# First layer of two more chunks by seven block products, with activations and weights parked in DRAM

## The chip, the cores and the metric

The kernel runs on one core of a Trainium2 chip. The metric is the device time of one execution in microseconds. Five engines run side by side, each through its own list of instructions in order: PE (matrix products; PEld is its weight load, which overlaps the products), DVE (VectorE), ACT (ScalarE), POOL (GpSimd) and SP, which here only issues DMA transfers. Engines wait for each other by semaphores.

## The reference

Masked attention over 8 batches and 8 heads of 576 tokens and 64 dimensions, then a feed-forward layer with softplus on the 4608 x 512 result:

```python
scores = scale * np.matmul(q, k.transpose(0, 1, 3, 2))
scores = np.where(masks, scores, -1000000000.0)   # local (32 wide) or strided (every 32nd), causal
scores = scores - np.max(scores, axis=-1, keepdims=True)
attn = np.exp(scores)
attn = attn / (np.sum(attn, axis=-1, keepdims=True) + 1e-09)
attn_out = np.matmul(attn, v)
x = attn_out.transpose(0, 2, 1, 3).reshape(4608, 512)
h = x @ w_in                                       # w_in 512 x 2048
g = np.maximum(h, 0.0) + np.log1p(np.exp(-np.abs(h)))
return g @ w_out                                   # w_out 2048 x 512
```

## The kernel before

**Precision by halves.** x, w_in, w_out and g are each kept as a high part in the fast 32-bit matmul type and a low part with the rest. A product is three matmuls: high x high, low weight x high, high weight x low.

**Tiling.** The tokens are 9 chunks (0 to 8) of 512, the 2048 hidden units 16 rows f of 128. For chunk c and row f the first layer, `hidden(c, f)` (L668), takes 4 blocks of the model dimension by 3, that is 12 matmuls of 128x512 into a bank `ph`. ACT makes absolute value, exponential and logarithm (L680, L683, L685), DVE the maximum and the sum, giving `u` (L689), then the high part `gh` (a cast, L267) and the low part `gl` (L708). The second layer, `output` (L719), takes 4 token tiles by 3 matmuls, into four banks `py` that collect over the 16 rows of a chunk. x sits in a ring of three chunks; all of w_in and w_out stays on chip.

**Attention** runs ahead of the chunks, by 32 head pairs (0 to 31, four to a batch): scores (L382), mask (L441), row maximum, subtraction, exponential, sums, division, 16 transposes on DVE (L496), the weighted sums with v (L564), and the split of x into parts (L600, L602). The scores of a pair and the weighted sums of the pair before stand together as one block on PE.

**Order.** The first stage, up to chunk 0, is a written list. After it a planner (class `Plan`) takes tasks with an engine, a cost, a due time and the tasks they follow, and writes one list for each engine. A step is one `hidden` and one `output`, two rows back. Letters in task names: F hidden, O output, S scores, V weighted sums, P transposes, L low part of x, P1 to P7 the block products, u softplus, h and l the parts of g, W the weight sums, X the x sums.

**Seven block products.** Chunks 7 and 8 are taken together. For two chunks and two rows f and f+8, a 2x2 block product by seven products instead of eight: a lap takes 7 products of 6 matmuls (L803). Sums of x blocks are made once, on DVE; sums of weight blocks are made earlier by the tasks W, stored to DRAM (`far`) and loaded for each lap into `ws` (L878). Products 1, 5 and 6 are copied out of their bank by ACT (`keep`, L882), and DVE adds the others to them (`join`, L887). Product P4 goes on adding in the bank that P7 has left, so it follows the join after P7. Eight laps make all 16 rows of both chunks, with the output tiles between the products.

Of the kernel before, what the change touches and what calls it, by code (L numbers as in the profile page):

```python
# [18 lines left out]
P = 128  # L19
# [97 lines left out]
def attention_softplus_ffn(  # L117
# [64 lines left out]

    def x_of(part, cc):
# [4 lines left out]
        return xs[part, cc]  # L188

# [33 lines left out]
    phs, us, ghs, gls, kept = {}, {}, {}, {}, {}  # L223
# [348 lines left out]
    def x_part(n, half, low):  # L572
# [85 lines left out]

    def hidden(c, f, pairs=range(NPAIR)):
# [4 lines left out]
        t0 = START[c] % RING  # L664
        i = 3 * pairs[0]
        for cc in (PAIRS[pair] for pair in pairs):
            for half, x in ((0, "h"), (1, "h"), (0, "l")):
                nc.tensor.matmul(  # L668
                    ph,
                    lhsT=w32["i", f][:, half, cc * P : (cc + 1) * P],  # L670
                    rhs=x_of(x, cc)[:, t0 : t0 + n],
                    start=(i == 0),
                    stop=(i == 3 * NCC - 1),
                )
                i += 1
# [11 lines left out]
    def softplus(c, f):  # L687
        u = us[c, f]
        nc.vector.scalar_tensor_tensor(  # L689
            u, in0=phs.pop((c, f)), scalar=0.0, in1=u, op0=ALU.max, op1=ALU.add  # L690
        )

    def g_high(c, f, engine=nc.vector):
        if c == NCHUNK - 1:
            kept[f] = w_pool.tile([P, 2, DM], F32R, tag=f"wi{f}", name=f"g_{c}_{f}")
            g = kept[f][:, 0]
        else:
            g = g_pool.tile([P, 512], F32R, tag="gh", name=f"gh_{c}_{f}")[:, : CH[c]]
        ghs[c, f] = g
        copy_on(engine, g, us[c, f])  # L700

    def g_low(c, f, engine):
        if c == NCHUNK - 1:
# [4 lines left out]
        engine.tensor_tensor(g, us.pop((c, f)), ghs[c, f].bitcast(F32), op=ALU.subtract)  # L708

    def y_of(c, t):  # L710

        return lend("b") if c == NCHUNK - 1 and t == 0 else py[t]

    def output(c, f, ts=None):
        gh, gl = ghs[c, f], gls[c, f]
        for t in ts or range(CH[c] // P):
            sl = slice(t * P, (t + 1) * P)
            for n, (g, half) in enumerate(((gh, 0), (gh, 1), (gl, 0))):
# [4 lines left out]
                    start=(f == 0 and n == 0),  # L723
                    stop=(f == NFC - 1 and n == 2),
# [12 lines left out]
    CA, CB = NCHUNK - 2, NCHUNK - 1  # L737
    at_a, at_b = START[CA] % RING, START[CB] % RING
    at_t = next(t for t in range(0, RING, 512) if t not in (at_a, at_b))
    assert CH[CA] == CH[CB] == 512  # L740
    lent, sums_r, sums_c = {}, {}, {}

    def lend(what):

        if what not in lent:
            if what == "ws":
                t = home(0, 4 * DM, "ws", F32R)
                lent[what] = t.rearrange("p (r x c) -> p r x c", r=2, x=2)
            elif what == "t1":
                t = home(1, 4 * DM, "t1", F32R)  # L750
                lent[what] = t.rearrange("p (i x c) -> p i x c", i=2, x=2)
            elif what in ("s1", "s2"):
                t = home(2, 2 * (PAD + S), "s12")
                lent["s1"], lent["s2"] = t[:, :DM], t[:, DM : 2 * DM]
            elif what == "s5":
                lent[what] = home(3, DM, "s5")
            elif what in ("a0", "b"):
                pool, tag = {"a0": (ps_s, "ps"), "b": (ps_o, "po")}[what]
                lent[what] = pool.tile([P, 512], F32, tag=tag, name=f"bank_{what}")
            else:  # L760
                lent[what] = ps_h.tile([P, 512], F32, tag="ph", name=f"bank_{what}")
        return lent[what]

    def x_at(part, k, lo):

        return x_of(part, k)[:, lo : lo + 512]

    def w_left(p, f, half, i):

        lo, hi = w32["i", f], w32["i", f + NFC // 2] if p == "4" else None  # L770
# [9 lines left out]
    def x_right(p, part, i):  # L780

        if p == "5":
            return lend("t1")[:, i, "hl".index(part)]
        k, lo = {
            "1": (i, at_a),
            "2": (2 + i, at_a),
            "3": (2 + i, at_b),
            "4": (2 + i, at_t),
            "6": (i, at_b),
            "7": (i, at_t),  # L790
        }[p]
        return x_at(part, k, lo)

    def bank_of(p, f):

        return lend({"2": "b", "5": "c", "3": "c"}.get(p, f"a{f % 2}"))

    def product(p, f):
        bank = bank_of(p, f)
        n = 0  # L800
        for i in range(2):
            for half, part in ((0, "h"), (1, "h"), (0, "l")):
                nc.tensor.matmul(  # L803
                    bank,
                    lhsT=w_left(p, f, half, i),
                    rhs=x_right(p, part, i),
# [6 lines left out]
    def x_whole(what, i, engine):  # L813

        k, lo = {"11": (i, at_a), "12": (i, at_b), "21": (2 + i, at_a), "22": (2 + i, at_b)}[what]
        if i == 1 and what in ("12", "21"):
            t = lend({"12": "s5", "21": "s2"}[what])
        else:
            t = io_pool.tile([P, DM], F32, tag="io", name=f"xw_{what}_{i}")
        sums_r[what, i] = t  # L820
        h, low = (x_at(part, k, lo).bitcast(F32) for part in "hl")
        engine.tensor_tensor(t, h, low, op=ALU.add)

    def x_sum(p, i, engine):

        out, plus, minus = {
            "5": ("11", "12", "11"),
            "7": ("12", "22", "12"),
            "6": ("22", "22", "11"),
            "4": ("21", "21", "22"),  # L830
        }[p]
        a, b, c = (sums_r[what, i] for what in (out, plus, minus))
        engine.tensor_tensor(a, b, c, op=ALU.subtract)
        sums_r[p, i] = a

    def x_sum_high(p, i):
        nc.scalar.copy(x_right(p, "h", i), sums_r[p, i])

    def x_sum_low(p, i):
        h = x_right(p, "h", i).bitcast(F32)  # L840
        nc.vector.tensor_tensor(x_right(p, "l", i), sums_r[p, i], h, op=ALU.subtract)
# [35 lines left out]
    def w_sum_load(r, f):  # L877
        nc.sync.dma_start(lend("ws")[:, r].bitcast(F32), far.pop((r, f)))  # L878

    def keep(s, p, f):  # L880

        nc.scalar.copy(lend(s), bank_of(p, f))  # L882

    def join(s, p, f, c, row):

        t = lend(s)
        nc.vector.tensor_tensor(t, bank_of(p, f), t, op=ALU.add)  # L887
# [142 lines left out]
    wanted = {}  # L1030
    for i, n in pair_at.items():
        b = order[n][0]
        for c in range(NCHUNK):
            if START[c] < (b + 1) * S and START[c] + CH[c] > b * S:
                wanted.setdefault(c, []).extend([f"L{n}0", f"L{n}1"])
    for i in range(begin, len(steps)):
        c, f = steps[i]
        w, x = CH[c] / 384, when[i]
        after = [f"F{i-1}", f"u{i-2}"] + wanted.get(c, [])
# [19 lines left out]
        for t in range(nt):  # L1059
# [4 lines left out]
            if f == NFC - 1:  # L1064
                e, cost, engine = (("ACT", 0.5, nc.scalar), ("DVE", 0.6, nc.vector))[t % 2]
                fn = lambda c=c, t=t, engine=engine: result(c, t, engine)
                add(f"y{k}.{t}", x + 0.7 * t + 0.7, e, cost, fn, [name])
    def sums_of(n):
        for half in range(2):
            weighted(n, half, n != last)  # L1070

    i_of = {n: i for i, n in pair_at.items()}
    for i, n in pair_at.items():
        x = when[i]
        if n > 2 * NPAIR:
            z = x - (when[i] - when[i - 2] if i - 2 in when else 0.0)
# [301 lines left out]
```

## Time and profile before

| what | value |
|---|---|
| runs | 871.91, 872.42, 873.01 us; median 872.42 |
| profiled execution | 872.67 us, span 870.6 |
| PE busy | 861.8 us (99%), 6578 matmuls |
| weight loads busy | 708.1 us (81%) |
| DVE busy | 646.8 us (74%) |
| ACT busy | 428.1 us (49%) |
| POOL busy | 65.8 us (8%) |
| DMA | 75.17 MB, mean 86 GB/s |

The span runs from the first to the last instruction. A busy matmul is shown from its issue to its modelled end, so matmuls overlap: what one costs is read from start to start. The chain of waits is followed back from the last instruction to whatever released each step.

### The profile page before, as it was taken

What the parts mean: (1) busy time and instruction counts of PE and PEld (TensorE: products, weight loads), DVE (VectorE), ACT (ScalarE), POOL (GpSimd) and SP (SyncE); (2) the same over time, 40 slices, a digit from 0 to 9 for tenths busy, and PEclk for the clock granted to TensorE, in tenths of its full rate; (3) what the DMA queues carried; (4) which work ended last, traced back from release to release, by engine and by line L of the source; (5) the groups of instructions that cost most, each with busy time, mean ns of one, the idle gap of its engine ahead of it and who ended that gap; (6) DMA issues with size and microseconds to landing.
All of it is one profiled execution on the core that took longest, in us unless ns stands there. A gap on an engine that the chain in (4) does not pass through costs nothing.

```text
span 870.6 us, 16405 instructions
## 1 busy us (share of the span) xinstructions
PE 861.8 (99%) x6578; PEld 708.1 (81%) x6578; DVE 646.8 (74%) x1395; ACT 428.1 (49%) x790; POOL 65.8 (8%) x88
## 2 busy tenths in 40 slices
PE   7999999999999999999999999999999999999998
PEld 6887888888888888888888888888888888888886
DVE  7999977888788788887788778887888765656500
ACT  6988754444444444444443443544443466656400
POOL 6346540000000000000000000000000000000000
PEclk9999999999999999999999999999999999999999
DMA  9893202211212221212212221212310122212010
GB/s 325 314 339 137 70 18 91 74 49 45 94 58 70 75 79 59 83 44 93 94 58 82 91 69 42 94 59 70 105 29 8 49 97 78 69 68 77 36 38 24
DMA packets 57003, 75.17 MB, mean 86 GB/s; under 512 B 3936, under 2 KB 36064, under 8 KB 56928
## 3 DMA queue, kind: packets, MB, share of 16 engines
q1 hardware_dynamic: 56640, 73.81, 25.6%
q8 instruction: 51, 0.84, 0.4%
q10 hardware_dynamic: 288, 0.33, 0.1%
q14 instruction: 24, 0.20, 0.1%
HBM read 56.30 MB, written 17.83 MB: 85 GB/s over the span
## 4 chain that ended last, share of the span: by engine, by line
PE 92%; DMA 3%; DVE 2%; ACT 1%; issue 1%; POOL 0%; SPq 0%; ACTq 0%; POOLq 0%
PE py L719 43%; PE ph L668 32%; PE bank_a L803 5%; PE bank_c L803 2%; DMA ri<-in_moe_w_in_dram 2%; PE ps L382 2%; PE pv L564 2%; PE po L564 2%; PE bank_b L719 1%; PE bank_b L803 1%; PE po L382 1%; DMA home<-in_v_dram 1%; DVE home L496 1%; PE pt L534 1%; DMA raw_q<-in_qk_dram 0%
## 5 line engine op out<-in xcount | busy, mean ns | idle before, releaser
L719 PE MATMUL py<-w_o,gh 128*128 128x512 f32 x1024 | 318.6, 392 | 0.0
L668 PE MATMUL ph<-x_h,w_i 128*128 128x512 f32 x896 | 276.8, 390 | 0.4 <-DVE u L689 0.4
L719 PEld LDWEIGHTS py<-w_o,gh 128*128 128x128 f32 x1024 | 190.1, 188 | 41.5
L680 ACT ACTIVATE u<-ph 128x512 f32<-128x512 f32 x112 | 66.8, 597 | 271.1 <-PE ph L668 268.6
L719 PE MATMUL py<-w_o,gl 128*128 128x512 f32 x512 | 199.3, 389 | 0.0
L668 PEld LDWEIGHTS ph<-x_h,w_i 128*128 128x128 f32 x896 | 167.5, 188 | 36.5 <-POOL home L485 0.8
L668 PE MATMUL ph<-x_l,w_i 128*128 128x512 f32 x448 | 174.3, 389 | 0.0
L496 DVE STREAM_TRANSPOSE home<-home 32x192 f32<-32x192 f32 x448 | 140.2, 317 | 6.9
L719 PEld LDWEIGHTS py<-w_o,gl 128*128 128x128 f32 x512 | 96.1, 188 | 20.3
L689 DVE SCALAR_TENSOR_TENSOR u<-ph,u 128x512 f32<-128x512 f32 x112 | 76.9, 687 | 34.6 <-ACT u L685 33.3
L668 PEld LDWEIGHTS ph<-x_l,w_i 128*128 128x128 f32 x448 | 84.1, 188 | 17.6
L683 ACT ACTIVATE u<-u 128x512 f32<-128x512 f32 x144 | 91.0, 633 | 4.1
L685 ACT ACTIVATE u<-u 128x512 f32<-128x512 f32 x144 | 91.0, 632 | 4.1
L708 DVE TENSOR_TENSOR gl<-u,gh 128x512 fp32r<-128x512 f32 x119 | 82.2, 691 | 7.9
L267 DVE CAST gh<-u 128x512 fp32r<-128x512 f32 x114 | 48.4, 424 | 7.9 <-PE py L719 0.5
L267 DVE COPY o<-py 128x512 f32<-128x512 f32 (+1 forms) x17 | 11.4, 670 | 50.8 <-PE py L719 50.8
L441 DVE TENSOR_TENSOR home<-ps,home 128x384 f32<-128x384 f32 x28 | 15.6, 556 | 34.2 <-PE ps L382 32.7
L267 ACT COPY home<-home 128x576 f32<-128x576 f32 x26 | 33.2, 1276 | 1.3 <-DMA home<-in_qk_dram 1.3
L456 ACT ACTIVATE home<-home 128x576 f32<-128x576 f32 x24 | 16.5, 688 | 34.6 <-DVE home L450 34.6
L680 ACT ACTIVATE u<-s 128x512 f32<-128x512 f32 x24 | 15.2, 633 | 36.9 <-DVE g L708 15.7
L719 PE MATMUL py<-w_o,g 128*128 128x512 f32 x144 | 32.8, 389 | 0.0
L719 PEld LDWEIGHTS py<-w_o,g 128*128 128x128 f32 x144 | 27.0, 188 | 5.6
(150 smaller groups left out, 917.6 us busy)
## 6 DMA issues: line engine op xcount, KB each, us to landing
home<-in_qk_dram SPq DMA_DIRECT2D x56, 288.0 KB, 2.9
home<-in_v_dram SPq DMA_DIRECT2D x28, 320.0 KB, 3.5
out_dram<-o SPq DMA_DIRECT2D x35, 256.0 KB, 2.1
ri<-in_moe_w_in_dram SPq DMA_DIRECT2D x16, 512.0 KB, 8.2
ro<-in_moe_w_out_dram SPq DMA_DIRECT2D x16, 512.0 KB, 8.7
ws<-far SPq DMA_DIRECT2D x16, 512.0 KB, 3.3
far<-wh SPq DMA_DIRECT2D x16, 256.0 KB, 2.4
far<-ww SPq DMA_DIRECT2D x16, 256.0 KB, 2.0
```

The lines of the kernel that those rows point to most:

```text
L267: (engine.copy if engine is nc.scalar else engine.tensor_copy)(dst, src)
L382: nc.tensor.matmul(pss[n, part][to : to + 32, at : at + 64], lhsT=qT[head, c : c + 32], rhs=k_of(n)[head, c : c + 64], start=True, stop=True,)
L496: nc.vector.transpose(pt[32 * (i + c) : 32 * (i + c) + 32, h, a : a + hi - lo, 32 * i : 32 * i + 32,], src[:, lo:hi, 32 * c : 32 * c + 32],)
L564: nc.tensor.matmul(po[64 * h : 64 * h + 64, TILE * x : TILE * x + TILE], lhsT=vs[n][:, a, h, :], rhs=pt_of(n, a)[:, h, a % 2], start=True, ...
L668: nc.tensor.matmul(ph, lhsT=w32["i", f][:, half, cc * P : (cc + 1) * P], rhs=x_of(x, cc)[:, t0 : t0 + n], start=(i == 0), stop=(i == 3 * N ...
L680: nc.scalar.activation(us[c, f], phs[c, f], AF.Abs)
L683: nc.scalar.activation(u, u, AF.Exp, scale=-1.0)
L685: nc.scalar.activation(u, u, AF.Ln, bias=1.0)
L689: nc.vector.scalar_tensor_tensor(u, in0=phs.pop((c, f)), scalar=0.0, in1=u, op0=ALU.max, op1=ALU.add)
L708: engine.tensor_tensor(g, us.pop((c, f)), ghs[c, f].bitcast(F32), op=ALU.subtract)
L719: nc.tensor.matmul(y_of(c, t), lhsT=g[:, sl], rhs=w32["o", f][:, half], start=(f == 0 and n == 0), stop=(f == NFC - 1 and n == 2),)
L803: nc.tensor.matmul(bank, lhsT=w_left(p, f, half, i), rhs=x_right(p, part, i), start=p in "125" and n == 0, stop=n == 5, skip_group_check=p ...
```

## The change

Chunks 5 and 6 are paired in the same way, for 7 of 8 laps; rows 7 and 15 of both stay plain. What that brings with it:

- Chunk 5's x has no room in the ring while chunks 6 and 7 are built, and gets a fourth place in the slots of w_in rows 12 to 15. The high and low blocks of w_in are stored to DRAM in chunk 1 (`w_store`). Rows 12 to 15, and 10 and 11 from chunk 3 on, are loaded back into two slots for each chunk 2 to 4 (`w_stream`).
- In both pairs each lap loads `near` (a row of w_in, 512 KB), `away` (half of another, 256 KB) and the two weight sums (512 KB each). The sums stay in DRAM for the second pair.
- The softplus results of chunk 6 are stored to DRAM (`u_store`) as they are made, and loaded back (`u_load`) for a stretch of chunk 6's outputs between the pairs.
- Attention pairs 8 to 27 come every third step. The scores of 28 to 31 stand at the ends of laps 0, 2, 4 and 6 of the new pair, the last weighted sums in the stretch of chunk 6's outputs.
- In the plain steps and for chunk 6 the cast to `gh` moves from DVE to ACT.
- The first lap of the new pair has one output tile between P7 and P4, since fewer tiles are at hand there.

```diff
+    PLACE = [0, 1, 2, 0, 1, 3, 2, 0, 1]
...
+    def w_store(f):
+        t = far_w[f] = far_pool.tile([P, 2, DM], F32, tag=f"farw{f}", name=f"far_w_{f}")
+        nc.sync.dma_start(t, w32["i", f].bitcast(F32))
+
+    def w_stream(c, f):
+        t = w_pool.tile([P, 2, DM], F32R, tag=f"wi{10+f%2}", name=f"w_i_{c}_{f}")
+        streamed[c, f] = t
+        nc.sync.dma_start(t.bitcast(F32), far_w[f])
...
+    def u_store(c, f):
+        t = far_u[c, f] = far_pool.tile([P, 512], F32, tag=f"faru{f}", name=f"far_u_{c}_{f}")
+        nc.sync.dma_start(t, us.pop((c, f)))
...
+    def w_sum_load(A, r, f):
+        nc.sync.dma_start(w_sums(A, r).bitcast(F32), far[r, f])
+
+    def w_near_load(A, f):
+        nc.sync.dma_start(w_near(A).bitcast(F32), far_w[f])
+
+    def w_away_load(A, f):
+        nc.sync.dma_start(
+            w_away(A)[:, 0].bitcast(F32), far_w[f + HALF][:, :, DM // 2 :]
+        )
...
-    steps = [(c, f) for c in range(CA) for f in range(NFC)]
+    NEAR = NCHUNK - 4
+    steps = [(c, f) for c in range(NEAR) for f in range(NFC)]
+    FAR0 = len(steps)
+    steps += [(NEAR, HALF - 1), (NEAR + 1, HALF - 1), (NEAR, NFC - 1)]
...
-    pair_at = {begin + 3 * i: 2 * NPAIR + i for i in range(NPAIR)}
-    for b in range(3, B):
-        for i in range(NPAIR):
-            pair_at[NFC * (b - 1) - 2 + (4 if b < B - 1 else 3) * i] = NPAIR * b + i
+    pair_at = {begin + 3 * i: n for i, n in enumerate(range(2 * NPAIR, far_first + 1))}
...
-        add(f"h{i}", x + 4.1, "DVE", 0.35 * w, lambda c=c, f=f: g_high(c, f), after)
+            add(f"h{i}", x + 4.1, "ACT", 0.65, lambda c=c, f=f: g_high(c, f, nc.scalar), after)
...
+            gaps = (1, 0, 0, 0, 1, 2) if f == 0 and A == NEAR else (1, 0, 1, 1, 3, 2)
+            some(gaps[0])
...
+    events = {(f, "scores"): far_first + 1 + k for k, f in enumerate((0, 2, 4, 6))}
+    lead = [(NEAR, NFC - 1, t) for t in range(TPC)]
+    laps = HALF - 1
+    pair_of_chunks(NEAR, lead, events, laps)
...
+    A = NCHUNK - 2
+    w_load(A, 0, now - 12)
+    x_task(A, now - 26, 1.2)
+    lead = [(C, g, t) for g in ROWS[C][-2:] for t in range(TPC)]
+    pair_of_chunks(A, lead, {}, HALF)
```

Three places of the order follow. A row is a line of the kernel, an operation, the tile written and the tiles read, with their numbers. First PE, from P7 to P4 in the first lap of a pair; before, it is that of chunks 7 and 8:

```order
L803 MATMUL bank_a0_7333<-x_h1_509,ws_7180 128x512 x2
L803 MATMUL bank_a0_7333<-x_l1_528,ws_7180 128x512
L719 MATMUL py3_109<-w_o_14_1464,gh_6_14_7326 128x512 x2
L719 MATMUL py3_109<-w_o_14_1464,gl_6_14_7328 128x512
L719 MATMUL py0_106<-w_o_15_1759,gh_6_15_7371 128x512 x2
L719 MATMUL py0_106<-w_o_15_1759,gl_6_15_7378 128x512
L719 MATMUL py1_107<-w_o_15_1759,gh_6_15_7371 128x512 x2
L719 MATMUL py1_107<-w_o_15_1759,gl_6_15_7378 128x512
L803 MATMUL bank_a0_7333<-x_h2_480,w_i_8_849 128x512 x2
```

Now, in the new pair of chunks 5 and 6 (`t_7` and `t_4` are the x sums for P7 and P4):

```order
L890 MATMUL bank_a_5_0_6130<-t_7_5_0_5950,ws_5_1_6037 128x512 x3
L890 MATMUL bank_a_5_0_6130<-t_7_5_1_6121,ws_5_1_6037 128x512 x3
L787 MATMUL py1_107<-w_o_15_1759,gh_5_15_6119 128x512 x2
L787 MATMUL py1_107<-w_o_15_1759,gl_5_15_6123 128x512
L890 MATMUL bank_a_5_0_6130<-t_4_5_0_6009,away_5_6127 128x512 x3
L890 MATMUL bank_a_5_0_6130<-t_4_5_1_6166,away_5_6127 128x512 x3
```

Three output tiles stood between the two products; one stands there now. Next SP, the loads of weight sums for laps 2 to 4 of the pair before:

```order
L878 DMA ws_7180<-far_0_2_4126 128x1024
L878 DMA ws_7180<-far_1_2_4185 128x1024
L878 DMA ws_7180<-far_0_3_4432 128x1024
L878 DMA ws_7180<-far_1_3_4505 128x1024
L878 DMA ws_7180<-far_0_4_5072 128x1024
L878 DMA ws_7180<-far_1_4_5131 128x1024
```

Now, in the new pair, for laps 2 and 3 (`home` is attention's q, k and v):

```order
L972 DMA near_5_5898<-far_w_2_1982 128x1024
L748 DMA far_u_6_8_6319<-kept_5_0_6168 128x512
L969 DMA ws_5_0_5392<-far_0_2_5437 128x1024
L969 DMA ws_5_1_6037<-far_1_2_5525 128x1024
L975 DMA away_5_6127<-far_w_10_2554 128x2x256
L972 DMA near_5_5898<-far_w_3_2066 128x1024
L748 DMA far_u_6_1_6434<-kept_5_1_6147 128x512
L284 DMA home_1_95<-in_qk_dram 128x576
L748 DMA far_u_6_9_6464<-kept_5_0_6168 128x512
L969 DMA ws_5_0_5392<-far_0_3_5737 128x1024
L969 DMA ws_5_1_6037<-far_1_3_5766 128x1024
L975 DMA away_5_6127<-far_w_11_2595 128x2x256
```

Two loads to a lap have become four, with two stores and attention's loads in the same list. Last DVE, where the x sums for chunks 7 and 8 are made; before, in the plain steps of chunk 6:

```order
L689 SCALAR_TENSOR_TENSOR u_6_10_7126<-ph_6_10_7092,u_6_10_7126 128x512
L267 CAST gh_6_10_7146<-u_6_10_7126 128x512
L708 TENSOR_TENSOR gl_6_10_7148<-u_6_10_7126,gh_6_10_7146 128x512
L833 TENSOR_TENSOR xw_11_0_6792<-xw_12_0_6982,xw_11_0_6792 128x512
L833 TENSOR_TENSOR xw_12_0_6982<-xw_22_0_6980,xw_12_0_6982 128x512
L833 TENSOR_TENSOR xw_22_0_6980<-xw_22_0_6980,xw_11_0_6792 128x512
```

Now, in the stretch of chunk 6's outputs:

```order
L772 TENSOR_TENSOR gl_6_10_7390<-u_6_1_7308,gh_6_10_7382 128x512
L922 TENSOR_TENSOR xw_7_0_7135<-xw_7_1_7328,xw_7_0_7135 128x512
L922 TENSOR_TENSOR xw_7_1_7328<-xw_7_1_7328,xw_7_0_7135 128x512
L772 TENSOR_TENSOR gl_6_3_7410<-u_6_2_7296,gh_6_3_7401 128x512
L932 TENSOR_TENSOR t_5_7_0_7289<-xw_7_0_7135,t_5_7_0_7289 128x512
L916 TENSOR_TENSOR xw_7_0_7135<-x_h2_480,x_l2_483 128x512
```

The softplus sum and the cast are gone from between them there (the sum was made in the laps, the cast is on ACT), and low parts of g and x sums alternate.

More of the change, by code (lines that the diff above doesn't have):

```diff
@@ L188, in x_of, with x_at @@
         return xs[part, cc]
+    def x_at(part, k, c):
+        place = PLACE[c]
+        if place < 3:
+            return x_of(part, k)[:, 512 * place : 512 * place + 512]
+        if k not in far_x:
+            far_x[k] = w_pool.tile([P, 2, DM], F32R, tag=f"wi{12+k}", name=f"x_far_{k}")
+        return far_x[k][:, "hl".index(part)]
     raw, w32 = {}, {}
@@ L656, in w_low, with w_i @@
         )
+    far_w, streamed = {}, {}
+    def w_store(f):
[5 more added lines that the diff above has]
+        nc.sync.dma_start(t.bitcast(F32), far_w[f])
+    def w_i(c, f):
+        for k in range(c, c - 3, -1):
+            if (k, f) in streamed:
+                return streamed[k, f]
+        return w32["i", f]
     def hidden(c, f, pairs=range(NPAIR)):
@@ L735, in result @@
         queue.dma_start(out[t0 : t0 + P, cols], o)
[L737 to L770, printed above, removed]
+    sums_r, sums_c, banks = {}, {}, {}
+    def slot(key, tag, shape, dtype=F32):
+        if key not in lent:
+            lent[key] = w_pool.tile(shape, dtype, tag=tag, name="_".join(map(str, key)))
+        return lent[key]
+    def half_of(key, tag, k):
+        return slot(key, tag, [P, 2, DM])[:, k]
+    def w_near(A):
+        return slot(("near", A), "wi10", [P, 2, DM], F32R)
@@ L780, in x_right @@
[L780 to L799, printed above, removed]
+            return w_away(A)[:, 0, half, at]
@@ L800, in product @@
+    def product(p, A, f):
+        bank = bank_of(p, A, f)
         n = 0
@@ L811, in product @@
                 n += 1
[L813 to L841, printed above, removed]
+    def stage(A, i, w):
+        k = {"a": 0, "b": 1, "c": 2}[w] + 3 * i
+        if A < NCHUNK - 2:
+            if i == 0:
+                return half_of(("xw", A, k // 2), f"wi{8+k//2}", k % 2)
+            if (A, w) not in sums_r:
+                sums_r[A, w] = io_pool.tile([P, DM], F32, tag="io", name=f"xw_{w}_{A}")
+            return sums_r[A, w]
+        return half_of(("xw", A, k // 2), f"wi{12+k//2}", k % 2)
@@ L1029, in attention_softplus_ffn, with lows_of @@
     add = plan.add
[L1030 to L1035, printed above, removed]
+    def lows_of(c):
+        return [
+            f"L{n}{half}"
+            for n in range(2 * NPAIR, len(order))
+            if START[c] < (order[n][0] + 1) * S and START[c] + CH[c] > order[n][0] * S
+            for half in range(2)
+        ]
     for i in range(begin, len(steps)):
@@ L1038, in attention_softplus_ffn @@
         w, x = CH[c] / 384, when[i]
[L1039 removed]
+        after = [f"F{i-1}", f"u{i-2}", f"G{c}.{f}"] + lows_of(c)
         if joint(i - 1):
@@ new lines, in needs_of, with parts_of @@
+    def needs_of(n):
+        return [f"Q{n}", f"k{n}", f"Y{n-1}0", f"Y{n-1}1", f"L{n-2}1"]
+    def parts_of(n, z, made):
+        first = order[n][0] * S
+        free = []
+        for c in range(NCHUNK):
+            if START[c] < first + S and START[c] + CH[c] > first:
+                old = [k for k in range(c) if PLACE[k] == PLACE[c]]
+                if old:
+                    free.append(f"F{NFC * old[-1] + NFC - 1}")
+                elif PLACE[c] == 3:
+                    free.append(f"F{2 * NFC - 1}")
+                    for g in range(12, NFC):
+                        free += [f"Wt{g}", f"W1.{g-HALF}"]
@@ L1117, in attention_softplus_ffn @@
         for half in range(2):
             z += 0.6
[L1120 to L1128 removed]
+            fn = lambda half=half: x_part(n, half, False)
@@ L1161, in out_task @@
             return
-        e, cost, engine = (("ACT", 0.6, nc.scalar), ("DVE", 0.7, nc.vector))[t % 2]
-        add(f"y{c}.{t}", now, e, cost, lambda: result(c, t, engine), [name])
+        e, cost, engine = (("ACT", 0.6, nc.scalar), ("DVE", 0.7, nc.vector))[t % 2 * (c > NEAR)]
+        add(f"y{c}.{t}", now, e, cost, lambda: result(c, t, engine), [name, *late])
+    g_users = [(NEAR - 1, NFC - 1), (NEAR, HALF - 1), (NEAR, NFC - 1)]
+    u_users = [f"Us{len(steps) - 2}", f"l{len(steps) - 1}"]
+    u_first = [f"A{len(steps) - 1}"]
@@ new lines, in g_room, with g_task @@
+    def g_room(c, f):
+        g_users.append((c, f))
+        old, g = g_users[-4]
+        if old == NEAR - 1:
+            return f"O{NFC * old + g}"
+        return f"O{old}.{g}.{TPC-1}"
+    def g_task(c, f, z, src, after):
+        n = f"{c}.{f}"
+        if c < NCHUNK - 1:
+            after = after + [g_room(c, f)]
+        e, cost, engine = ("ACT", 0.65, nc.scalar) if c in SPILLED else ("DVE", 0.45, nc.vector)
+        add(f"h{n}", z, e, cost, lambda: g_high(c, f, engine), [src] + after)
+        add(f"l{n}", z + 0.5, "DVE", 0.75, lambda: g_low(c, f, nc.vector), [f"h{n}"])
@@ new lines, in soft_task @@
+            after = [src, u_users[-2], u_first[-1]] if step == 0 else [f"A{step-1}.{n}"]
+            add(f"A{step}.{n}", z + step, "ACT", 0.65, fn, after)
+        u_first.append(f"A0.{n}")
+        add(f"u{n}", z + 3, "DVE", 0.75, lambda: softplus(c, f), [f"A2.{n}"])
+        if c in SPILLED:
+            u_users.append(f"Us{n}" if (c, f) in PLAIN else f"u{n}")
+            add(f"Us{n}", z + 4, "SP", 0.8, lambda: u_store(c, f), [f"u{n}"], 2.5)
+        else:
+            u_users.append(f"l{n}")
+            g_task(c, f, z + 3.7, f"u{n}", list(late))
@@ new lines, in attention_softplus_ffn @@
+    for k, g in enumerate(ROWS[C][:-2]):
+        if k == 7:
+            name = f"V{last}"
+            free = [f"j{j}.{NEAR}.{laps-1}" for j in "12"]
+            after = [chain, f"P{last}", f"v{last}", *free]
+            add(name, now, "PE", 1.3, lambda: sums_of(last), after)
+            parts_of(last, now + 1.3, name)
+            push(name, 6.4)
+        for t in range(TPC):
+            out_task(C, g, t)
+    A = NCHUNK - 2
+    w_load(A, 0, now - 12)
+    x_task(A, now - 26, 1.2)
+    lead = [(C, g, t) for g in ROWS[C][-2:] for t in range(TPC)]
```

580 lines of the change are left out of this document (384 added, 196 removed).

## The prediction

> **What bounds the kernel now.** I read the head of the page first, then the busy times per stretch, then the PE timeline around attention blocks and around the block products.
>
> ```profile
> span 870.6 us, 16405 instructions
> PE 861.8 (99%) x6578; PEld 708.1 (81%) x6578; DVE 646.8 (74%) x1395; ACT 428.1 (49%) x790; POOL 65.8 (8%) x88
> PE 92%; DMA 3%; DVE 2%; ACT 1%; issue 1%; POOL 0%; SPq 0%; ACTq 0%; POOLq 0%
> core 0: 870.6 us, clock 1.000
> ```
>
> PE is busy in 99% of the span and is 92% of the chain of waits; the DMA, VectorE and ScalarE shares belong to the first stage, which the change leaves alone. A modelled busy time can hide slack, so the next question is whether PE's pitch is its own. In the windows below the columns are length, then busy us and (count) of PE, PEld, DVE, ACT, POOL, then clock, DMA share, GB/s.
>
> ```profile
> 701.55:716.51 14.96, 14.96 (x67) 12.39 (x66) 8.52 (x15) 8.67 (x16) 0.00 (x0) 1.00 0.41 141
> 716.51:731.47 14.96, 14.96 (x67) 12.39 (x66) 9.87 (x18) 8.78 (x15) 0.00 (x0) 1.00 0.22 71
> 820.00:860.00 40.00, 40.00 (x179) 33.10 (x178) 3.39 (x6) 2.35 (x4) 0.00 (x0) 1.00 0.13 46
> 168.99:187.67 18.68, 18.68 (x169) 15.36 (x169) 15.15 (x37) 8.15 (x15) 0.00 (x0) 1.00 0.20 54
> 629.56:648.24 18.68, 18.68 (x169) 15.36 (x168) 16.57 (x38) 8.06 (x13) 0.00 (x0) 1.00 0.08 22
> ```
>
> The first two are one lap each of the seven block products of chunks 7 and 8: 66 weight loads and matmuls in 14.96 us, 0.2267 us each. The third is the second layer's end, where DVE is busy 3.4 us of 40 and ACT 2.4: 40.00/178 = 0.225, the same pitch to 1%. So nothing but PE sets it, and a matmul that disappears takes 0.2267 us with it, as long as the others stay in step. The last two are three plain steps with one attention pair; even the heavier, with DVE at 16.57 of 18.68 us (89%), has PE unbroken. These are the measure for VectorE below.
>
> **The change part by part.**
>
> *Removed matmuls.* Seven laps replace fourteen rows of the first layer in chunks 5 and 6. A plain row takes 12 matmuls, two chunks and two rows 48; seven products of 6 take 42. So 7 x 6 = 42 matmuls of 128x512 go, and the instruction order of PE shows just these 42 fewer. 42 x 0.2267 = **-9.52 us**.
>
> [...]
>
> *Attention on PE.* The pairs move to other places, with as many matmuls; but pair 27's weighted sum and pair 28's scores, one joint block before, are now two.
>
> ```profile
> 302.49 0.39 PE L668 MATMUL ph<-x_l,w_i 128*128 128x512 f32 x1
> 304.94 0.73 PE L719 MATMUL py<-w_o,gh 128*128 128x512 f32 x2
> 132.47 0.39 PE L668 MATMUL ph<-x_l,w_i 128*128 128x512 f32 x1
> 133.77 0.73 PE L719 MATMUL py<-w_o,gh 128*128 128x512 f32 x2
> 672.04 0.39 PE L668 MATMUL ph<-x_l,w_i 128*128 128x512 f32 x1
> 672.36 1.21 PE L564 MATMUL pv<-home,home 128*64 128x96 f32 x24
> 673.50 0.74 PE L719 MATMUL py<-w_o,gh 128*128 128x512 f32 x2
> 704.27 0.62 PE L719 MATMUL py<-w_o,gh 128*128 128x512 f32 x2
> ```
>
> From the start of the last wide matmul to the next output, less one pitch: joint 2.45 - 0.23 = 2.22 us, scores alone 1.07, weighted alone 1.23. One split costs 1.07 + 1.23 - 2.22 = 0.08, and the first two output matmuls after a block take 0.73 where 0.62 is usual, 0.11 more for each return: **+0.2 us**.
>
> *Lap 0 of the new pair.* In it one output tile (three matmuls, 0.68 us) stands between P7 and P4, where a lap of the old pair has three. P4 adds on to the bank that P7 has left, so it waits for the join that reads that bank on DVE.
>
> ```profile
> 738.04 0.39 PE L803 MATMUL bank_a<-x_l,ws 128*128 128x512 f32 x1
> 738.47 0.69 DVE L887 TENSOR_TENSOR s<-bank_a,s 128x512 f32<-128x512 f32 x1 [0.68 <-PE bank_a L803]
> 740.31 0.62 PE L803 MATMUL bank_a<-x_h,w_i 128*128 128x512 f32 x2
> ```
>
> From the start of P7's last matmul to the join's end is 739.16 - 738.04 = 1.12 us. PE reaches P4 0.23 + 0.68 = 0.91 us after that start. The stall is 0.21 us and a hand-over of some hundredths: **+0.25**. In the other laps three tiles give 2.27 us, and it is covered.
>
> *VectorE and ScalarE in chunks 1 to 4.* Attention pairs come every third step now instead of every fourth, and eight weight-sum tasks fall here. Per plain step DVE does the rows below once.
>
> ```profile
> L689 DVE SCALAR_TENSOR_TENSOR u<-ph,u 128x512 f32<-128x512 f32 x112 | 76.9, 687 | 34.6 <-ACT u L685 33.3
> L708 DVE TENSOR_TENSOR gl<-u,gh 128x512 fp32r<-128x512 f32 x119 | 82.2, 691 | 7.9
> L267 DVE CAST gh<-u 128x512 fp32r<-128x512 f32 x114 | 48.4, 424 | 7.9 <-PE py L719 0.5
> L267 ACT CAST gh<-u 128x512 fp32r<-128x512 f32 x11 | 6.6, 613 | 1.4 <-DVE u L689 1.0 <-PE py L719 0.5
> L680 ACT ACTIVATE u<-ph 128x512 f32<-128x512 f32 x112 | 66.8, 597 | 271.1 <-PE ph L668 268.6
> L496 DVE STREAM_TRANSPOSE home<-home 32x192 f32<-32x192 f32 x448 | 140.2, 317 | 6.9
> L887 DVE TENSOR_TENSOR s<-bank_a,s 128x512 f32<-128x512 f32 x8 | 5.5, 691 | 5.1 <-PE bank_a L803 5.1
> ```
>
> A three-step stretch was 15.15 us on DVE. Three casts go to ACT, -1.27; a weight-sum task, two whole sums and two low parts at 0.69 and four sums at 0.42, is 4.45 us and comes twice in 16 steps, +1.67; copies of results +0.25. That is 15.8 of 18.68 us, below the 16.57 that ran unbroken. ACT goes from 8.15 to about 10.5. Cost 0; without that cover a shortfall would be the excess itself. At steps 6 to 9 of chunk 4 two tasks and a pair coincide, and I count 18.9 against 18.68; but DVE is ahead:
>
> ```profile
> 200.82 2.58 DVE L496 STREAM_TRANSPOSE home<-home 32x192 f32<-32x192 f32 x8
> 206.34 0.48 PE L382 MATMUL ps<-home,home 64*32 64x64 f32 x20
> ```
>
> The last transposes end at 203.40, 2.9 us before the block that reads them. So this should be absorbed, and I take **+0.2** for small slips of this kind, between 0 and 1.
>
> *The laps of the new pair.* Two laps with one joint attention block are 2 x 14.96 + 2.34 = 32.3 us of PE. DVE does three joins, four softplus ends, two casts and two low parts in each, 3 x 0.691 + 4 x 0.687 + 2 x 0.424 + 2 x 0.691 = 7.05, and one attention pair: 15.15 less three steps of 1.80 leaves 9.75. Together 23.9, 74%. Hidden.
>
> *Loads.* Each lap takes four loads (two of weight sums and a near block of 512 KB each, an away block of 256 KB) and two stores of softplus results of 256 KB, all on SP, in order. The last two columns of the issue rows are size and time to landing.
>
> ```profile
> ws<-far SPq DMA_DIRECT2D x16, 512.0 KB, 3.3
> far<-wh SPq DMA_DIRECT2D x16, 256.0 KB, 2.4
> ri<-in_moe_w_in_dram SPq DMA_DIRECT2D x16, 512.0 KB, 8.2
> ro<-in_moe_w_out_dram SPq DMA_DIRECT2D x16, 512.0 KB, 8.7
> L878 SPq DMA_DIRECT2D ws<-far x16: 319/319/424, 673.7 to 798.3; - x16
> DMA to landing us min/median/max: 3.0/3.3/4.6
> ```
>
> A lap runs P1, P2, output tile, P5, P6, tile, P3, tile, P7, three tiles, P4, two tiles, at 1.36 us a product and 0.68 a tile. The tightest load is the second weight-sum tile: its place is free after P7, at 10.20, and P5 of the next lap reads it at 14.96 + 3.40 = 18.36. That leaves 8.16 us for an issue of 0.32 and a landing of 3.3 to 4.6. The near block has 12.2 us after P2, the away block 13.6 after P4. On SP the weight sums stand behind the two stores, and these wait for softplus results:
>
> ```profile
> 741.44 0.39 PE L803 MATMUL bank_a<-x_l,w_i 128*128 128x512 f32 x1
> 744.07 0.69 DVE L689 SCALAR_TENSOR_TENSOR u<-bank_a,u 128x512 f32<-128x512 f32 x1 [0.59 <-ACT u L685]
> ```
>
> From P4's end to the last result of a lap it is 744.76 - 741.83 = 2.93 us, so a store is gone by about 3 us into the next lap, far ahead of 10.20. A lap moves 2.36 MB in 14.96 us, 158 GB/s, beside 141 in the first window, which held such loads and no stall. In chunks 2 to 4 each streamed block of weights is issued when its place's last reader is done, three blocks of twelve matmuls or 8.16 us ahead. Cost 0; if the cover is gone, the price is in the second rival.
>
> *Outputs of chunk 6.* After the laps PE makes two output blocks of chunk 5, 14 of chunk 6 and pair 31's weighted sums with no first layer beside them, 16 x 2.72 + 0.8 = 44.3 us. DVE has 16 low parts (11.1), 24 sums and low parts of x for the next pair (24 x 0.69 = 16.6), pair 31 (9.75) and the laps' tail (2.2): 39.6 us, 89%, the same as in the heaviest window above. Hidden, but thin.
>
> **Sum.** The profiled run took 872.67 us (span 870.6 and 2.07 around it). 872.67 - 9.52 + 0.20 + 0.25 + 0.20 = 863.80; the median of the runs, 872.42, is 0.25 below the profiled one, so **863.5 us**.
>
> **The rivals.**
>
> *VectorE late in the outputs of chunk 6.* Each low part now follows a cast on another engine. DVE takes its instructions in order, so where the cast is not ready it stands for up to 0.61 and about 0.5 of hand-overs. If that happens at eight of the sixteen, 39.6 + 8.8 = 48.4 against 44.3 and some 0.4 of lead: +3.7, **867.2 us**. For it: 89% busy without these waits. Against: the 16.57-in-18.68 window also had casts and lows and no stall, though there the cast was DVE's own and brought no hand-over; that is what stays open.
>
> *Loads late, slower than before.* If landings in the laps are not the 3.3 us of the old laps but the 8.2 to 8.7 of the first stage, the second weight-sum tile comes 0.32 + 8.7 = 9.02 us after P7, 0.86 after P5 wants it. Thirteen laps have such a load ahead of them (six of the new pair, seven of the old). It decides from a landing of 7.84, and the gain of 8.9 is spent at 0.69 a lap, a landing of 8.5. At 8.7: 863.5 + 13 x 0.86 = **874.7 us**; where the near block's landing delays its sibling too, more. For it: 158 GB/s in every lap, where the old laps had 141 once and then 70. Against: the first stage, where landings were that long, moved over 300.
>
> ```profile
> GB/s 325 314 339 137 70 18 91 74 49 45 94 58 70 75 79 59 83 44 93 94 58 82 91 69 42 94 59 70 105 29 8 49 97 78 69 68 77 36 38 24
> ```
>
> *A removed matmul is worth less than its pitch.* PEld is busy for 81%, and if only a weight load's time, 12.39/66 = 0.188 us, went with each matmul, 42 x 0.188 = 7.9 us would be saved and the time be **865.1 us**. But the pitch is 0.227 in every window, with DVE busy or not, so this gets little. [...]
>
> *No less work, or the gain given back.* That the 42 matmuls are still there is excluded by PE's order. That many small stalls in DVE's and ACT's crowded steps sum to some 8 us, and the time is about 872, is possible, with no single place to name.
>
> **How the numbers follow.** Forecast 0.72 (its own range 862.3 to 864.9: slips of 0 to 1, and the half microsecond by which the runs differ), matmuls worth less 0.03, VectorE late 0.11, gain given back 0.05, loads late 0.09. The range for 8 in 10 takes the first three, 862.3 to 868.3. What can be told from no change is 0.2%, 1.74 us: faster means below 870.7, as in the first three, 0.86; within it 0.05; slower 0.09.
>
> **What would show it.** Right: PE has 42 fewer wide matmuls, laps of 14.96 us (17.3 with an attention block), one gap of about 0.25 us at P4 of the first lap, and PE idle nowhere else after 75 us. VectorE late: gaps of PE before output blocks of chunk 6, released by the low parts. Loads late: gaps before P5 that a landing of weight sums ends, and landings over 7.8 us. Wrong altogether: laps longer than 15 us with no wait shown, which would say that the pitch is not PE's own.

## The result

The changed kernel takes 864.41 us (864.06 to 865.16); the kernel before 872.48 on the same chip. The ratio is 0.9909, 95% interval 0.9892 to 0.9926. Timed once more, it is 863.44 us and 0.9900 (0.9885 to 0.9915). The forecast was 863.5 us. The head of the page after, with busy time per engine and the chain of waits:

```profile
span 863.1 us, 16559 instructions
PE 853.4 (99%) x6536; PEld 700.7 (81%) x6536; DVE 640.9 (74%) x1370; ACT 492.2 (57%) x913; POOL 65.9 (8%) x88
...
PE 92%; DVE 4%; ACT 2%; issue 1%; DMA 0%; POOL 0%; ACTq 0%; POOLq 0%
```

PE has 42 instructions fewer (6536 for 6578) and is still busy 99% of the span. The windows answer to those of before: two laps of the new pair with one attention block, then the stretch of chunk 6's outputs.

```profile
548.57:580.84 32.27, 32.27 (x234) 26.62 (x228) 23.93 (x49) 21.72 (x36) 0.00 (x0) 1.00 0.58 184
645.40:689.75 44.35, 44.35 (x215) 36.54 (x214) 34.86 (x67) 19.09 (x35) 0.00 (x0) 1.00 0.40 121
```

Both are as long as PE's own work there, 32.3 and 44.3 us by the prediction. The loads of 512 KB landed as fast as the old ones, 3.3 us in the median in both. The stores of softplus results took 3.6 us in the median, where the stores of weight sums, as large, took 2.4 and 2.0 in the kernel before (size, then median us to landing):

```profile
ws<-far SPq DMA_DIRECT2D x30, 512.0 KB, 3.3
...
near<-far_w SPq DMA_DIRECT2D x15, 512.0 KB, 3.3
...
away<-far_w SPq DMA_DIRECT2D x15, 256.0 KB, 3.0
far_u<-kept SPq DMA_DIRECT2D x14, 256.0 KB, 3.6
```

**The first stage must be set apart.** It is the same work in both kernels (975 matmuls, 167 instructions on VectorE and 162 on ScalarE up to the mark below), and it does not end at the same time in every execution. A fixed mark is the first wide matmul behind the first joint attention block. Before, after, and after in the second profile:

```profile
85.28 0.73 PE L668 MATMUL ph<-x_h,w_i 128*128 128x512 f32 x2
```

```profile
86.32 0.73 PE L718 MATMUL ph<-x_h,w_i 128*128 128x512 f32 x2
```

```profile
84.53 0.73 PE L718 MATMUL ph<-x_h,w_i 128*128 128x512 f32 x2
```

From that mark to the span's end it is 870.6 - 85.28 = 785.3 us before, 776.8 after, and 776.9 after again (its span is 861.4). So the change is worth 8.5 us behind the mark, by one trace of the kernel before and two of the changed one, and the first stage moves single executions by up to a microsecond to either side. Times below are compared behind the mark where tenths matter.

### The profile page after: what moved, and what is told of

Its sections match the earlier page's. It is cut to its first block, busy times and chain, and to the rows that moved or that the text cites. A ratio compares the mean times of both kernels' runs of the same rounds, so it can differ in the third digit from the quotient of the medians.

```text
span 863.1 us, 16559 instructions
## 1 busy us (share of the span) xinstructions
PE 853.4 (99%) x6536; PEld 700.7 (81%) x6536; DVE 640.9 (74%) x1370; ACT 492.2 (57%) x913; POOL 65.9 (8%) x88
## 4 chain that ended last, share of the span: by engine, by line
PE 92%; DVE 4%; ACT 2%; issue 1%; DMA 0%; POOL 0%; ACTq 0%; POOLq 0%
PE py L787 43%; PE ph L718 23%; PE bank_a L890 10%; PE bank_c L890 5%; PE bank_b L890 2%; PE pv L584 2%; PE ps L402 2%; PE po L584 2%; PE py_last L787 1%; PE po L402 1%; PE pt L554 1%; DVE home L516 1%; DVE a_i L672 0%; DVE a_o L672 0%; DMA raw_q<-in_qk_dram 0%
## 5 line engine op out<-in xcount | busy, mean ns | idle before, releaser
L718 PE MATMUL ph<-x_h,w_i 128*128 128x512 f32 x656 | 202.8, 390 | 0.5 <-DVE u L742 0.5
L718 PEld LDWEIGHTS ph<-x_h,w_i 128*128 128x128 f32 x656 | 122.6, 188 | 26.7 <-POOL home L505 0.9
L718 PE MATMUL ph<-x_l,w_i 128*128 128x512 f32 x328 | 127.7, 389 | 0.0
L287 ACT CAST gh<-u 128x512 fp32r<-128x512 f32 x89 | 55.2, 621 | 107.7 <-DVE u L742 84.7
L730 ACT ACTIVATE u<-ph 128x512 f32<-128x512 f32 x84 | 50.1, 598 | 90.8 <-PE ph L718 88.2
L718 PEld LDWEIGHTS ph<-x_l,w_i 128*128 128x128 f32 x328 | 61.6, 188 | 13.0
L742 DVE SCALAR_TENSOR_TENSOR u<-ph,u 128x512 f32<-128x512 f32 x84 | 57.7, 687 | 13.7 <-ACT u L735 12.5
L730 ACT ACTIVATE u<-kept 128x512 f32<-128x512 f32 x45 | 28.4, 631 | 41.1 <-DVE kept L986 25.6
L986 DVE TENSOR_TENSOR kept<-bank_c,kept 128x512 f32<-128x512 f32 x15 | 10.4, 692 | 33.8 <-PE bank_c L890 33.8
L287 ACT COPY o<-py 128x512 f32<-128x512 f32 (+1 forms) x21 | 11.5, 574 | 38.4 <-PE py L787 27.6
L981 ACT COPY kept<-bank_a 128x512 f32<-128x512 f32 x30 | 17.6, 586 | 25.8 <-PE bank_a L890 24.2
```

Of the source, the lines that this page charges most:

```text
L287: (engine.copy if engine is nc.scalar else engine.tensor_copy)(dst, src)
L718: nc.tensor.matmul(ph, lhsT=w_i(c, f)[:, half, cc * P : (cc + 1) * P], rhs=x_at(x, cc, c), start=(i == 0), stop=(i == 3 * NCC - 1),)
L730: nc.scalar.activation(us[c, f], phs[c, f], AF.Abs)
L742: nc.vector.scalar_tensor_tensor(to, in0=ph, scalar=0.0, in1=u, op0=ALU.max, op1=ALU.add)
```

## The experiments

**The change again.** No edit.

> The changed kernel once more, unaltered, for a closer interval and a second trace of the first stage. In the profiled run of the change PE had one gap after the first stage, in the first lap of the new pair, but that run's first stage ended 1.0 us later than in the run before. Theory A (the first stage varies from run to run, the change does not touch it): this trace's first stage ends within half a microsecond of the one before the change, or on its other side, and the time is 863.5 to 864.5 us. Theory B (the change lengthens the first stage): the first stage ends about 1 us later again, and the median is above 864.4.

Measured: 863.44 us, with the mark at 84.53. Theory A holds. Over all ten profiles of changed kernels here the mark lies between 84.25 and 86.32, so the 1.0 us by which the first profile ended its first stage later is nothing that the change did.

**42 matmuls put back.**

```diff
-        for i in range(2):
+        last = 11 if p == "2" and A == NEAR else 5
+        for i in (0, 1, 0, 1)[: (last + 1) // 3]:
...
-                    stop=n == 5,
+                    stop=n == last,
```

> In the seven laps of the new pair the product P2 is computed twice into its bank (the sum there is then twice P2, so chunk 5's results are others): 42 matmuls of 128x512 more, nothing else altered. Theory A (PE sets the pace, a matmul is worth its pitch of 0.2267 us): 42 x 0.2267 = +9.5 us, 873.9. Theory B (a matmul is worth only its weight load, 0.188 us): +7.9, 872.3. [...]

Measured: 873.88 us, ratio 1.0017 (1.0008 to 1.0027). Two laps with an attention block, as above:

```profile
547.86:582.85 34.99, 34.99 (x246) 28.88 (x240) 23.92 (x49) 21.71 (x36) 0.00 (x0) 1.00 0.52 171
```

34.99 - 32.27 = 2.72 us for twelve matmuls, 0.2267 each. Behind the mark 870.6 - 84.25 = 786.35, 9.5 us more than the change. By the clock it is 9.5 us more than 864.41 and 10.4 more than 863.44, so the tenths come from the trace alone. Theory A holds; a price of 0.188 us, 7.9 for the 42, is out.

**98 matmuls taken away.** The third term of each product in the new pair is left out.

```diff
-            for half, part in ((0, "h"), (1, "h"), (0, "l")):
+            terms = ((0, "h"), (1, "h"), (0, "l"))[: 2 if A == NEAR else 3]
+            for half, part in terms:
...
-                    stop=n == 5,
+                    stop=n == 2 * len(terms) - 1,
```

> In the seven laps of the new pair every product leaves out its third term (high weight x low x), 14 matmuls a lap, 98 in all; the results lose that part of the precision. It takes PE's cover away from VectorE: a lap is 52 matmuls, 11.8 us instead of 14.96, and two laps with an attention block 26.0 instead of 32.3, with 23.9 us of VectorE work (92%). Theory A (VectorE and the loads were hidden with room to spare): 98 x 0.2267 = -22.2 us less a little, 842 to 846, with gaps of PE in the laps that hold attention. Theory B (the laps are already close to what VectorE or the loads allow): less than half of it, 853 or above, with PE waiting in every lap.

Measured: 846.89 us. Behind the mark 844.8 - 84.61 = 760.2, 16.7 us less of the 22.2 that went. It just misses theory A's range and is far from B's. PE's waits (total, times, longest) and four laps of the pair with two attention blocks, 52.0 us by the expectation:

```profile
PE bank_a L891 <- ACT kept L982: 2.4, 3, 0.8
...
PE bank_b L891 <- DVE home L461: 0.8, 1, 0.8
PE bank_c L891 <- ACT kept L982: 0.5, 1, 0.5
```

```profile
543.55:597.80 54.25, 51.88 (x377) 41.31 (x376) 45.74 (x95) 42.24 (x72) 0.00 (x0) 1.00 0.65 215
```

What gives first is not VectorE's sum of work, 45.7 us and under 52.0, but hand-overs. P7 waits for ScalarE's copy of P6, which stands in ScalarE's list behind softplus steps that wait for VectorE:

```profile
564.10 0.63 ACT L730 ACTIVATE u<-kept 128x512 f32<-128x512 f32 x1 [0.40 <-DVE kept L742]
564.64 0.57 ACT L982 COPY kept<-bank_a 128x512 f32<-128x512 f32 x1
```

P2 waits for the mask to be added in the bank it shares with the scores. On VectorE the mask stands behind a softplus step, which waits for ScalarE, which has waited for a store of a softplus result to read its tile:

```profile
543.32 0.63 ACT L730 ACTIVATE u<-kept 128x512 f32<-128x512 f32 x1 [2.45 <-DMA far_u<-u]
...
545.31 0.69 DVE L742 SCALAR_TENSOR_TENSOR kept<-kept,u 128x512 f32<-128x512 f32 x1 [2.53 <-ACT u L735]
545.91 0.55 DVE L461 TENSOR_TENSOR home<-ps,home 128x384 f32<-128x384 f32 x1
```

PE waited for no load. From start to start PE's waits, with the slower matmuls right behind each (four in 1.20 us at 546.52, where four take 1.07 without a wait), cost 5.2 us of the 5.5.

**Two output tiles before P4 in the first lap.** First the rows of the change there: P7, the join, the one tile's last matmul, P4.

```profile
542.32 1.52 PE L890 MATMUL bank_a<-t,ws 128*128 128x512 f32 x6
...
543.88 0.69 DVE L986 TENSOR_TENSOR kept<-bank_a,kept 128x512 f32<-128x512 f32 x1 [0.60 <-PE bank_a L890]
544.13 0.39 PE L787 MATMUL py<-w_o,gl 128*128 128x512 f32 x1
...
544.63 0.73 PE L890 MATMUL bank_a<-t,away 128*128 128x512 f32 x2
```

P4 starts at 544.63, the join ends at 544.57; without a wait P4 would start at 544.36. It is the one gap of PE behind the first stage that exceeds 0.2 us, measured as time beyond the pitch.

```diff
-            gaps = (1, 0, 0, 0, 1, 2) if f == 0 and A == NEAR else (1, 0, 1, 1, 3, 2)
+            gaps = (1, 0, 0, 0, 2, 1) if f == 0 and A == NEAR else (1, 0, 1, 1, 3, 2)
```

> In the first lap of the new pair two output tiles stand between P7 and P4 instead of one, and one behind P4 instead of two. Theory A (P4 waits there for the join after P7, 0.27 us, and the pipeline refills for 0.13 more): PE reaches P4 1.59 us after the start of P7's last matmul, the join is done at 1.2, the gap goes and the time falls by 0.4 us, which is below what the timing can tell but shows in the trace. Theory B (the gap has another cause, such as the away block's load): a gap of about 0.3 us stays at P4.

```profile
543.60 0.39 PE L787 MATMUL py<-w_o,gl 128*128 128x512 f32 x1
543.82 1.52 PE L890 MATMUL bank_a<-t,away 128*128 128x512 f32 x6
```

The gap is gone: 0.22 us from start to start, and six matmuls in 1.52 us instead of a slow first pair. Behind the mark 861.5 - 85.12 = 776.4, 0.4 to 0.5 us less than the change. By the clock, 863.64 us, it can't be told from it. Theory A holds, and this is the better version, if by little.

**The casts of the plain steps back on VectorE.**

```diff
-            add(f"h{i}", x + 4.1, "ACT", 0.65, lambda c=c, f=f: g_high(c, f, nc.scalar), after)
+            add(f"h{i}", x + 4.1, "DVE", 0.45, lambda c=c, f=f: g_high(c, f), after)
```

> One part of the change undone: in the plain steps the cast to the high part goes back from ScalarE to VectorE, the planner orders the rest anew. From 86 to 480 us VectorE was busy 331.5 of 394 us with the cast on ScalarE; some 60 casts at 0.424 make it 357, 91%. Theory A (VectorE had room; the denser attention did not need the cast moved): within 0.5 us of the change, 863 to 864.5. Theory B (the moved cast carries part of the gain): at the steps with a weight-sum task and an attention pair, where I counted 18.9 of 18.68 us without the cast, each is about 1.3 us over; eight such places would cost up to 10 us, and 2 to 6 after the lead VectorE has: 866 to 870.

Measured: 864.82 us, ratio 0.9910 (0.9893 to 0.9928).

```profile
86.00:480.00 394.00, 393.57 (x3448) 322.96 (x3447) 350.93 (x818) 191.97 (x361) 22.34 (x22) 1.00 0.37 120
```

```profile
PE py L787 <- DVE o L287: 0.4, 1, 0.4
```

VectorE is busy 89%, and one wait is longer than before: an output bank is copied out late, because the copy stands behind transposes. 863.1 - 85.51 = 777.6 behind the mark, 0.7 to 0.8 us more. So the moved cast is worth that and no more. The time is just above theory A's range and below B's.

**The casts of chunk 6 on VectorE.**

```diff
-        e, cost, engine = ("ACT", 0.65, nc.scalar) if c in SPILLED else ("DVE", 0.45, nc.vector)
+        e, cost, engine = "DVE", 0.45, nc.vector
```

> For chunk 6, whose activations come back from DRAM, the cast to the high part goes from ScalarE to VectorE. In the 44.35 us of output blocks between the pairs VectorE was busy 34.85 us and stood 8.2 us at eleven low parts that waited for their cast, 43.05 together, and PE had no gap. Theory A (waiting and casting are exchanged): 16 casts at 0.424 are 6.8 us, the 8.2 of waits go, VectorE needs 41.6 and the time stays within 0.5 us, 863 to 864.5. Theory B (VectorE is late, the first rival of the prediction): the casts come on top, 49.9 against 44.35, PE waits at output blocks, +3 to +5 us, 867 to 869.

In the change VectorE stood at low parts in this stretch for (total, times, longest):

```profile
DVE gl L772 <- ACT gh L287: 8.2, 11, 1.4
```

With the casts on VectorE the same stretch reads:

```profile
643.99:688.34 44.35, 44.35 (x215) 36.53 (x214) 39.42 (x80) 9.59 (x18) 0.00 (x0) 1.00 0.37 121
```

Measured: 863.46 us, and PE has no gap here. Theory A holds: waits were exchanged for casts. The in-order waits of the first rival happen, 8.2 us of them, and cost nothing.

**Weight sums loaded later.** In the laps the loads are issued behind the away block's.

```diff
-                free = [f"P{p}.{A}.{f-1}" for p in used]
+                free = [f"P{p}.{A}.{f-1}" for p in used] + [f"Wb.{A}.{f}"]
```

> On SP the two loads of weight sums of a lap are put behind the load of the away block, which waits for P4: they are issued 3.4 to 4.2 us later than P7 allows, some 4 us before P5 reads the first. The computation is the same. Theory A (landings of 3.2 us with a longest of 4.8, slack of 4.5 us before): the slack shrinks to about 0.6 us, the time rises by 0 to 3 us, only where a landing is long or another load stands ahead in the queue. Theory B (the loads were close to late): 13 laps lose most of the 3.4 us, +30 us or more.

Measured: 878.66 us, ratio 1.0078 (1.0056 to 1.0100), some 15 us more than the change, and between the theories. The trace is of the longest of its four executions, 881.77 us; the others took 878 to 879. The time to landing of the weight sums (least, median, most), and PE's waits for them:

```profile
DMA to landing us min/median/max: 3.1/5.1/7.0
```

```profile
PE bank_c L890 <- DMA ws<-far: 6.6, 5, 3.4
...
PE bank_a L890 <- DMA ws<-far: 1.9, 5, 0.5
```

The delay alone would fit theory A: the expectation leaves some 4 us before P5 reads the first sum, enough for a landing of 3.3. But the three loads, 1280 KB, are now issued together, and the landing goes from 3.3 to 5.1 us. So here a landing wasn't a constant of a transfer's size: it grew with what was issued beside it. No run has the delay without the loads together, so their shares are argued. The spacing of the loads by their different release points, P2, P3, P7 and P4, is part of what makes the change work.

**More traffic, behind the near block.**

```diff
         nc.sync.dma_start(w_near(A).bitcast(F32), far_w[f])
+        spare = far_pool.tile([P, 2, DM], F32, tag=f"spare{A}{f}", name=f"spare_{A}_{f}")
+        nc.sync.dma_start(spare, far_w[f + HALF])
```

> Each lap of both pairs copies another 512 KB within DRAM, behind the near block's load on the same queue: 1 MB more read and written a lap of 15 us, on top of 2.4 MB in the new pair. Nothing waits for the copy. Theory A (transfers are far from a limit): landings of the weight sums grow by at most 2 us, to about 5, below the 7.84 at which PE would wait, and the time is unchanged within 0.5 us. Theory B (loads late, the slower rival of the prediction): landings pass 8 us, 0.5 to 1 us a lap is lost, +6 to +13.

Measured: 868.39 us, ratio 0.9954 (0.9938 to 0.9970), 4 to 5 us more than the change. The size lies between the theories, at most 0.5 by A and 6 to 13 by B, and the place is neither's: the weight sums landed in 3.3 us, at most 4.4. Beside the gap of the first lap PE lost time twice, 1.6 and 1.8 us, at P7. SP's and ScalarE's rows around the first:

```profile
564.98 0.33 SPq L972 DMA_DIRECT2D near<-far_w  x1
565.36 0.49 SPq L974 DMA_DIRECT2D spare<-far_w  x1
565.90 0.57 SPq L748 DMA_DIRECT2D far_u<-kept  x1
```

```profile
571.89 0.59 ACT L983 COPY kept<-bank_a 128x512 f32<-128x512 f32 x1 [2.56 <-DMA far_u<-kept]
```

P7 adds to the bank of P6 and waits for ScalarE to copy P6 out. The copy goes to the tile that holds the softplus result of the lap before, until its store to DRAM has read it. The store is queued behind the near block, here also behind the spare copy, and lands about 6 us later. In the change itself, in the same lap of its second profile:

```profile
565.28 0.35 SPq L748 DMA_DIRECT2D far_u<-kept  x1
...
569.49 0.59 ACT L981 COPY kept<-bank_a 128x512 f32<-128x512 f32 x1 [0.30 <-DMA far_u<-kept]
...
570.76 1.52 PE L890 MATMUL bank_a<-t,ws 128*128 128x512 f32 x6
```

The copy waits 0.30 us there too, and ends at 570.08, 0.7 us before P7 starts. That is a thin cover, and a transfer has a part in it. In the first lap the copies ahead of P6 and P7 end 0.57 us before them, with no transfer involved.

**The same traffic, behind the away block.**

```diff
             w_away(A)[:, 0].bitcast(F32), far_w[f + HALF][:, :, DM // 2 :]
         )
+        spare = far_pool.tile([P, 2, DM], F32, tag=f"spare{A}{f}", name=f"spare_{A}_{f}")
+        nc.sync.dma_start(spare, far_w[f + HALF])
```

> The same 512 KB copy within DRAM in each lap as in the run with the doubled traffic, but put on SP behind the away block's load instead of behind the near block's, about 4 us before the near block and the store of the softplus result are issued. With the copy behind the near block, PE lost 1.6 and 1.8 us in two laps at P7: ScalarE's copy of P6 writes the tile whose store to DRAM had not yet been read out, and the store stood behind the spare copy. Theory A (the store's place in the queue is the thin spot, not the traffic): the store lands as in the change, at most 4.5 us after its issue, P7 does not wait, 863 to 864.5 us. Theory B (the added bytes by themselves slow the laps): again about +4 to +5 us, 867 to 869, wherever the copy stands.

Measured: 864.35 us, ratio 0.9911 (0.9895 to 0.9928).

```profile
PE bank_a L890 <- ACT kept L983: 0.5, 1, 0.5
```

```profile
ACT kept L983 <- DMA far_u<-kept: 1.9, 2, 1.6
```

As many bytes cost 0.8 us behind the mark (862.8 - 85.17 = 777.6) instead of 3.7 (865.3 - 84.76 = 780.5, against 776.8). Two laps of this run moved 225 GB/s without a gap of PE, and two of the run with the copy behind the near block 202 with one. Theory A holds in the main: the store's place in the queue decides. The traffic isn't wholly free: a store took up to 5.5 us to land, where theory A had at most 4.5, and P7 waited half a microsecond for one.

## Why the prediction was right

- **42 matmuls, -9.52 us.** Right: behind the mark the change is -8.5 net, and 42 put back cost 9.5. The pitch carried the sum, and the rival of a lower worth falls with the same run.
- **One split of an attention block, +0.2.** Right: in both traces the blocks cost 2.22, 1.08 and 1.23 us, and each return 0.13, so the split is +0.22.
- **Lap 0, +0.25.** The place and the cause were right, the size was short: 0.27 us of gap and 0.13 more until the matmuls are at their pitch again, 0.40.
- **Small slips, +0.2.** One place is seen, 0.13 us at 334.6, where an output bank waited for its copy on VectorE, between steps with transposes. The crowded steps of chunk 4 that the prediction named show no wait. A further 0.3 us lies where the prediction had no term: in each of the last four output tiles, behind 821 us, some ten matmuls around those that read `g_home` and `away` stand 0.230 to 0.241 us apart, and the same ones do in both traces of the change. One of them, 0.24 us from start to start:

```profile
857.78 0.40 PE L787 MATMUL py<-w_o,away 128*128 128x512 f32 x1
858.02 1.32 PE L787 MATMUL py<-w_o,g 128*128 128x512 f32 x5
```

  The trace shows no wait there, and why these are slower is open.
- **Sum.** -9.52 + 0.40 + 0.22 + 0.13 + 0.30 = -8.47 behind the mark; measured -8.5. The prediction's own terms come to -8.87, so the work behind the mark gained 0.4 us less than forecast. That the second median, 863.44, lies on the forecast of 863.5 is luck in part: in its profile the first stage ended 0.75 us earlier than in the profile of the kernel before. The rest of the distance to the two medians is the first stage's spread.
- **VectorE in the laps and in chunks 1 to 4: hidden.** Right; 23.9 us for two laps was forecast and 23.93 measured.
- **VectorE in the outputs of chunk 6: hidden but thin.** Hidden, but not with the load forecast: 39.6 us were counted and 34.86 measured. Above all the x sums were counted too high, 24 for 16.6 us where 21 for 13.2 stand in the stretch, and the laps' tail, 2.2 where 0.9 is left. The rival's waits of 8.8 us were nearly met, 8.2, and still it did not come, since 34.9 + 8.2 is under 44.35. By the rival's own sum 39.6 + 8.2 would have been over it, so luck had a part. But waits and work are exchanged in part: with 39.42 of real work, in the run with these casts on VectorE, PE had no gap either.
- **Loads: hidden, the weight sums the tightest.** The result was right, the step was not. The weight sums were named as the tightest transfer; the tightest that the runs show is the store of the softplus result, since the next lap's copy of P6 writes the tile it reads. The prediction followed the store only until it is issued, to see that the loads behind it are not held, and did not ask who waits for its landing. In the lap shown, 0.7 us are left between that copy and P7. And the landing of 3.3 us, against which the weight sums' cover was set, holds for the order as it is: issued together with the away block they took 5.1 us in the median and up to 7.0.

## What to carry to other kernels

Where PE's pitch is the same in stretches with idle and with loaded neighbours, 0.225 and 0.2267 us here, expect a removed matmul to be worth that pitch, as the 42 put back were with 9.5 us, and ask which cover breaks first. For each new transfer ask for both ends: what its landing feeds, and which tile it keeps occupied until it has been read; here the store of a softplus result, with 0.7 us of cover, was more urgent than any load. Leave loads spread over a lap by their release points: issued together, the weight sums landed in 5.1 us instead of 3.3. And put what nobody waits for behind those that something does: the spare copy cost 3.7 us behind the near block, 0.8 behind the away block.

## What had not been expected of the hardware

- Traffic in the laps went from 71 to 141 GB/s in the windows before to 184, and the median landing of 512 KB stayed at 3.3 us; three loads issued together raised it to 5.1.
- When the late loads held PE for 3.4 us at one place, the granted clock read 1.00 for 2.5 us behind the end of the last matmul and then 0.50 for 6.8 us. It is the third number from the end:

```profile
714.26:716.75 2.49, 0.00 (x1) 0.00 (x0) 2.42 (x6) 1.89 (x3) 0.00 (x0) 1.00 0.97 348
716.75:723.58 6.83, 5.93 (x14) 4.68 (x15) 1.74 (x4) 0.99 (x2) 0.00 (x0) 0.50 0.33 121
```

```profile
717.65 2.92 PE L890 MATMUL bank_c<-t,ws 128*128 128x512 f32 x6 [3.38 <-DMA ws<-far]
```

The six matmuls that follow take 2.92 us instead of 1.52, and with those up to 724 us the one wait cost about 2.9 us beyond itself. The run that lost 1.6 and 1.8 us at P7 kept a granted clock of 1.000. A stretch as long without a matmul did not always bring a fall: behind the last matmul of the span the clock read 1.00 to the end, for 3.53 us in the changed kernel and 3.65 in the one before:

```profile
859.57:863.10 3.53, 0.00 (x0) 0.00 (x0) 0.43 (x1) 0.37 (x1) 0.00 (x0) 1.00 0.22 74
```

```profile
866.95:870.60 3.65, 0.00 (x1) 0.00 (x0) 0.42 (x1) 0.37 (x1) 0.00 (x0) 1.00 0.21 72
```

Why the clock fell in the one place and not in the others, the runs do not show.
